# Moving 256 columns at a time in a feed-forward: every wide matmul split in two, and its operands placed anew

## The chip, the cores and the metric

The kernel runs on one core of a Trainium2 chip. The metric is the device time of one execution in microseconds; the median of three runs is shown below. All work is in float32, or in float32 values that are split into an upper part (the value rounded to the matmul type float32r) and a lower part (the rest), so that three float32r matmuls give one product of nearly full precision.

## The reference

Linear attention without a softmax, a root-mean-square norm with a gain, and a feed-forward with SiLU on the 4608 tokens:

```python
kv = np.einsum('bhsd,bhse->bhde', k, v)          # q, k, v: 8 batches, 8 heads, 576 tokens, 64
out = np.einsum('bhsd,bhde->bhse', q, kv)
rms = np.sqrt(np.mean(out * out, axis=-1, keepdims=True) + 1e-06)
x = (out / rms * g_norm).transpose(0, 2, 1, 3).reshape(4608, 512)
h = x @ w_in                                     # 512 x 2048
y = (h / (1 + np.exp(-h))) @ w_out               # 2048 x 512
```

## The kernel before

The tokens are cut into nine blocks of 512 (TN), and the hidden units into 16 groups of 128 (NF), called f. Both weight matrices stay in SBUF as blocks wi0 to wi15 and wo0 to wo15, each with its upper and lower part side by side. Attention for a later batch runs between the feed-forward's steps. The order in which instructions are issued on each engine is that of the program (a manual schedule); jobs of attention are hung on steps by hand.

For each block of tokens and each group f the kernel makes the hidden units (128 units on the partitions, 512 tokens as columns), gates them, and adds their part of the output.

- Blocks 0 and 1: `products` (line 474) makes the hidden units. For each of four quarters c of the 512 inputs, three matmuls: stationary a 128 x 128 piece of wi, moving 512 columns of x. Block 0's x lies in four tiles x0 to x3 (three in "spare" places, x3 in a "late" place), block 1's in x_second.
- Blocks 2 to 8: `pair_step` makes two groups at once with seven Strassen-like products. `product` (line 634) issues six matmuls for each, with 256 moving columns of an operand tile (operands 0 to 3 lie over x_second's place, 4 to 6 in the spare places). A pair step has 42 of these.
- All blocks: `project` (line 505) adds a group's part of the output. Stationary is a 128 x 128 piece of the gated units (gh, the upper part, or gl, the lower), moving are 512 columns of wo. For each of the block's four output tiles of 128 tokens it issues three matmuls: gh by the lower part of wo, gh by its upper part, and gl by the upper part. In the last block the fourth output tile is held in two half banks, so these move 256 columns each. A pair step issues 24 of the wide ones for the two groups of an earlier step (two steps behind).

The gated units are allocated in the pool gp, the weights in the pool weights. Constants and x lie in the pool const, in the order in which they are first asked for. Where a tile starts is therefore set by what stands ahead of it. The kernel before already places one pair of operands on purpose: one tile x_place holds x_second from its start, and the operands of `product` 48 floats (192 bytes) further on.

```python
SHIFT = 48
x_place = const.tile([P, NP * 2 * TN + SHIFT], F32R, name="x_place")
x_second = x_place[:, :NP * 2 * TN].rearrange("p (c a n) -> p c a n", c=NP, a=2)
x_operands = x_place[:, SHIFT:].rearrange("p (c a k n) -> p c a k n", c=NP, a=2, k=2)
```

In this text the distance of a matmul is the start of its moving operand less the start of its stationary operand, modulo 256 bytes.

At the start, `keep_warm` (line 824) issues small matmuls of 128 columns on an identity while the first loads are under way, and GpSimd makes constants: four zeroed tiles, the identity, a permuted identity called both, and the column warm_up that ScalarE reads first.

Of the kernel before, what the change touches and what calls it, by code (L numbers as in the profile page):

```python
# [8 lines left out]
F32 = mybir.dt.float32  # L9
F32R = mybir.dt.float32r  # L10
# [20 lines left out]
def linear_attention_rms_silu_ffn(  # L31
# [22 lines left out]
    nc = tc.nc  # L54
    B, NP, P, S = q.shape
# [3 lines left out]
    TN = 512  # L59
# [5 lines left out]
    const = ctx.enter_context(tc.tile_pool(name="const", bufs=1))  # L65
# [5 lines left out]
    gp = ctx.enter_context(tc.tile_pool(name="gp", bufs=LAG + 1))  # L71
# [2 lines left out]
    ps_at = ctx.enter_context(tc.tile_pool(name="ps_at", bufs=1, space=PSUM))  # L74
    dram = ctx.enter_context(tc.tile_pool(name="dram", bufs=1, space=bass.MemoryType.DRAM))

    kvm = [const.tile([P, P], F32, name=f"kvm{i}") for i in range(NP)]
    for t in kvm:
        nc.gpsimd.memset(t, 0.0)
    ident = const.tile([P, P], F32, name="ident", tag="kh", bufs=2)  # L80
    make_identity(nc, ident)
    warm_up = const.tile([P, 1], F32, name="warm_up")
    nc.gpsimd.memset(warm_up, 1.0)
    gcol = const.tile([P, 1], F32, name="gcol")
    both = const.tile([P, P], F32, name="both", tag="kl", bufs=2)
    nc.gpsimd.tensor_copy(out=both, in_=ident)
    for i in range(4):
        nc.gpsimd.tensor_copy(
            out=both[32 * i:32 * i + 32, 32 * (i ^ 1):32 * (i ^ 1) + 32], in_=ident[32 * i:32 * i + 32, 32 * i:32 * i + 32]
        )  # L90
    d_eps = const.tile([P, 1], F32, name="d_eps")
    nc.gpsimd.memset(d_eps, float(D) * EPS)

    def load_g():
        for h in range(P // D):
            nc.sync.dma_start(out=gcol[h * D:(h + 1) * D, :], in_=g_norm.rearrange("(d o) -> d o", o=1))
# [7 lines left out]

    SHIFT = 48
    x_place = const.tile([P, NP * 2 * TN + SHIFT], F32R, name="x_place")
    x_second = x_place[:, :NP * 2 * TN].rearrange("p (c a n) -> p c a n", c=NP, a=2)
    x_operands = x_place[:, SHIFT:].rearrange("p (c a k n) -> p c a k n", c=NP, a=2, k=2)  # L110
    x_first, lates = {}, {}

    def spare(n, shape, dtype, name):
        return const.tile(shape, dtype, name=name, tag=f"spare{n}")

    def late(n, shape, dtype, name):
        if not lates:
            const.tile([P, 64 - SHIFT], F32, name="gap")
        if name not in lates:
            lates[name] = const.tile(shape, dtype, name=name, tag=f"late{n}")  # L120
        return lates[name]

    def x32(c, w):

        return late(c // 2, [P, 2, TN], F32, f"x32_{c // 2}")[:, c % 2, w]
# [14 lines left out]
    def full_tile(kind, f):  # L140
        if kind == "wo":
            t = late(1, [P, 2, NP * P], F32, "wo_full")[:, f % 2]
        else:
            t = tmp.tile([P, S], F32, name="full", tag="tmp")[:, :NP * P]
        fulls[kind, f] = t
        return t
# [54 lines left out]
    def x_part(t, a, c):  # L201

        if t == 1:
            return x_second[:, c, a]
        if c not in x_first:
            kind = {"shape": [P, 2, TN], "dtype": F32R, "name": f"x{c}"}
            x_first[c] = spare(c, **kind) if c < 3 else late(0, **kind)
        return x_first[c][:, a]
# [248 lines left out]
    def h_bank():  # L457
        return ps_h.tile([P, 512], F32, name="hp", tag="h")
# [6 lines left out]
    def at_bank(tag=None):  # L465

        at_tags.append(at_tags.pop(0))
        return ps_at.tile([P, 512], F32, name="at", tag=tag or at_tags[-1])

    def products(hp, t, f, c):  # L470
        w = parts["wi", f]
        fs = slice(c * P, (c + 1) * P)
        for i, (a, b) in enumerate(((0, 1), (1, 0), (0, 0))):
            nc.tensor.matmul(  # L474
                out=hp[:, :TN], lhsT=w[:, a, fs], rhs=x_part(t, b, c),
                start=(c == 0 and i == 0), stop=(c == NP - 1 and i == 2),
            )

    def gate(t, hp):
# [19 lines left out]
    def project(t, f, gh, gl, bank, n, cs):  # L499
        first, last = order(t)[0], order(t)[-1]  # L500
        w = parts["wo", f]
        ns = slice(n * P, (n + 1) * P)
        bank = bank[:, :cs.stop - cs.start]
        for i, (g, a) in enumerate(((gh, 1), (gh, 0), (gl, 0))):
            nc.tensor.matmul(  # L505
                out=bank, lhsT=g[:, ns], rhs=w[:, a, cs], start=(f == first and i == 0), stop=(f == last and i == 2)
            )
        if f == last:
            ob = tmp.tile([P, S], F32, name="ob", tag="tmp")[:, :cs.stop - cs.start]
            (nc.scalar.copy if n % 2 else nc.vector.tensor_copy)(out=ob, in_=bank)  # L510
            nc.sync.dma_start(out=out[t * TN + n * P:t * TN + (n + 1) * P, cs], in_=ob)
# [9 lines left out]
    def order(t):  # L521

        if t < 2:
            return [(f + t * HF) % NF for f in range(NF)]
        return [f for i in range(HF) for f in (i + HF, i)]
# [69 lines left out]
    def operand(j):  # L595

        if j < 4:
            return x_operands[:, j]
        if j not in operands:
            operands[j] = spare(j - 4, [P, 2, 2, H], F32R, f"operand{j}")  # L600
        return operands[j]
# [20 lines left out]
    def make_operand(m):  # L622
        j, x, _ = seven[m]
        upper, lower = operand(j)[:, 0], operand(j)[:, 1]
        nc.scalar.copy(out=upper, in_=x())
        nc.vector.tensor_tensor(out=lower, in0=x(), in1=upper.bitcast(F32), op=ALU.subtract)

    def product(m, i, out):
        j, _, a_of = seven[m]
        x = operand(j)  # L630
        n = 0
        for c in range(2):
            for a, b in ((0, 1), (1, 0), (0, 0)):
                nc.tensor.matmul(  # L634
                    out=out, lhsT=a_of(i, a, c), rhs=x[:, b, c], start=(n == 0), stop=(n == 5)
                )
                n += 1
# [11 lines left out]
    def pair_step(t, i, groups):  # L649
# [5 lines left out]
        def due(n):  # L655
            while n > 0 and groups:
                n -= (groups[0][-1].stop - groups[0][-1].start) / DM
                project(*groups.pop(0))
# [144 lines left out]
    with tc.manual_schedule():  # L803

        first = [FirstPair(c) for c in range(NP)]
        stats = at_bank().rearrange("p (c i j) -> p c i j", i=2, j=8)
        second = plan(1, 3)
        for item in ORDER.split():
            kind, n = item.rstrip("0123456789"), int(item.lstrip("wiopbg") or 0)
# [30 lines left out]
        def warm_products(c, *fs):  # L840
            if not warm:
                warm.extend([h_bank(), acc_bank()])
            for f in fs:
                products(warm[f], 0, f, c)
# [115 lines left out]
        for t in range(NT):  # L960
# [7 lines left out]
            for step, f in enumerate(order(t)):  # L968
                g = t * NF + step
                for job in first_jobs.pop(g, ()):  # L970
                    job()
                for item in prepped:
                    split_block(*item, nc.scalar.copy)
                prepped = []
                if t == 0:
                    prepped = [("wi", f + 2)] * (3 <= f + 2 < NF) + [("wo", f)] * (f > 0)
                run(sum((bits(*item) for item in prepped), []), *[call() for call in chains.pop(g, ())])
                if t == 0 and 3 < f + 3 < NF:
                    magnitude("wi", f + 3)
                if t == 0 and f < WARM:  # L980
                    hp = warm[f]
                    products(hp, t, f, NP - 1)
                else:
                    hp = h_bank()
                    for c in range(NP):
                        products(hp, t, f, c)
                pend.append(((t, f, *gate(t, hp)), sums))
                if t == 0 and f + 1 < NF:
                    magnitude("wo", f + 1)
                for job in mid_jobs.pop(g, ()):  # L990
                    job()
                if len(pend) > LAG:
                    item, olds = pend.pop(0)
                    for old in olds:
                        project(*item, *old)
                for job in last_jobs.pop(g, ()):
                    job()
# [4 lines left out]
        for old in sums:  # L1002
            for item, _ in pend:
                project(*item, *old)
# [41 lines left out]
```

## Time and profile before

| | before |
|---|---|
| median of 3 runs | 839.12 us (838.94 to 839.2) |
| the profiled execution: its own time | 839.63 us |
| the profiled execution: its span | 837.8 us |
| TensorE matmuls busy | 826.8 us, 5454 instructions |
| TensorE weight loads busy | 734.6 us, 5454 instructions |
| VectorE busy | 528.9 us |
| ScalarE busy | 359.0 us |
| GpSimd busy | 145.9 us |

The span goes from the first to the last instruction; the time of an execution is a little longer. Weight loads overlap the matmuls. Matmuls are pipelined, so the rows of two matmuls that follow each other overlap as well, and the mean length of a row is not what one matmul adds to the time. In the views of the chain of waits a run of matmuls is given from its start to the start of what follows it.

### The profile page before, as it was taken

What the parts mean: (1) busy time and instruction counts of PE and PEld (TensorE: products, weight loads), DVE (VectorE), ACT (ScalarE), POOL (GpSimd) and SP (SyncE); (2) the same over time, 40 slices, a digit from 0 to 9 for tenths busy, and PEclk for the clock granted to TensorE, in tenths of its full rate; (3) what the DMA queues carried; (4) which work ended last, traced back from release to release, by engine and by line L of the source; (5) the groups of instructions that cost most, each with busy time, mean ns of one, the idle gap of its engine ahead of it and who ended that gap; (6) DMA issues with size and microseconds to landing.
All of it is one profiled execution on the core that took longest, in us unless ns stands there. A gap on an engine that the chain in (4) does not pass through costs nothing.

```text
span 837.8 us, 14032 instructions
## 1 busy us (share of the span) xinstructions
PE 826.8 (99%) x5454; PEld 734.6 (88%) x5454; DVE 528.9 (63%) x1027; ACT 359.0 (43%) x744; POOL 145.9 (17%) x142
## 2 busy tenths in 40 slices
PE   8999999999999999999999999999999999999998
PEld 7767888888899999998999998999999999999997
DVE  4886875788476567657766667656865664464332
ACT  3766564534453245325532355225532432243222
POOL 2786983423010002000200011001100000000000
PEclk9999999999999999999999999999999999999999
DMA  8879011337343634364424452444423343334331
GB/s 322 313 257 362 4 57 51 136 145 261 122 161 100 215 115 146 101 214 144 165 91 160 163 173 88 158 158 157 151 84 103 106 155 103 105 102 151 100 102 51
DMA packets 42418, 122.55 MB, mean 146 GB/s; under 512 B 4848, under 2 KB 5104, under 8 KB 42352
## 3 DMA queue, kind: packets, MB, share of 16 engines
q1 hardware_dynamic: 42352, 121.65, 42.4%
q8 instruction: 43, 0.70, 0.4%
q14 instruction: 23, 0.19, 0.1%
HBM read 103.81 MB, written 17.83 MB: 145 GB/s over the span
## 4 chain that ended last, share of the span: by engine, by line
PE 94%; DMA 4%; POOL 1%; ACT 0%; issue 0%; SPq 0%
PE acc L505 46%; PE hp L634 33%; PE hp L474 9%; PE at L253 2%; DMA k<-in_k 1%; DMA wo<-in_moe_w_out 1%; DMA early_wi<-in_v 1%; DMA v<-in_v 1%; PE at L289 1%; PE at L288 1%; PE at L290 1%; PE at L505 1%; DMA wi<-in_moe_w_in 1%; PE at L286 1%; POOL wo L191 0%
## 5 line engine op out<-in xcount | busy, mean ns | idle before, releaser
L505 PE MATMUL acc<-wo,gh 128*128 128x512 f32 (+1 forms) x1152 | 354.1, 389 | 0.1
L505 PEld LDWEIGHTS acc<-wo,gh 128*128 128x128 f32 x1152 | 210.3, 188 | 39.7 <-POOL wo L191 0.3
L505 PE MATMUL acc<-wo,gl 128*128 128x512 f32 x576 | 223.0, 387 | 0.5 <-POOL gl L485 0.5
L634 PE MATMUL hp<-x_place,wi 128*128 128x256 f32 x1344 | 167.8, 280 | 0.0
L634 PEld LDWEIGHTS hp<-x_place,wi 128*128 128x128 f32 x1344 | 162.0, 189 | 0.0
L634 PEld LDWEIGHTS hp<-operand,wi 128*128 128x128 f32 x1008 | 126.0, 189 | 3.9
L505 PEld LDWEIGHTS acc<-wo,gl 128*128 128x128 f32 x576 | 108.1, 188 | 23.5 <-POOL gl L485 0.9
L634 PE MATMUL hp<-operand,wi 128*128 128x256 f32 x1008 | 127.5, 281 | 0.0
L275 POOL TENSOR_TENSOR ql<-q,qh 128x576 fp32r<-128x576 f32 x24 | 35.6, 1483 | 376.0 <-ACT qh L274 341.9
L685 ACT COPY wi<-hp 128x256 f32<-128x256 f32 x56 | 20.9, 373 | 140.9 <-PE hp L634 140.9
L643 ACT ACTIVATE gh<-gf 128x512 fp32r<-128x512 f32 x56 | 35.4, 633 | 94.4 <-DVE gf L698 81.6
L643 ACT ACTIVATE gh<-wi 128x512 fp32r<-128x512 f32 x56 | 35.5, 634 | 79.8 <-DVE wi L698 68.0
L686 DVE TENSOR_TENSOR gf<-hp,wi 128x256 f32<-128x256 f32 x28 | 11.9, 425 | 84.8 <-ACT wi L685 84.8
L686 DVE TENSOR_TENSOR wi<-hp,wi 128x256 f32<-128x256 f32 x28 | 11.9, 424 | 84.3 <-ACT wi L685 84.3
L474 PE MATMUL hp<-x,wi 128*128 128x512 f32 x180 | 46.4, 402 | 1.4 <-POOL wi L191 1.4
L474 PE MATMUL hp<-x_place,wi 128*128 128x512 f32 x192 | 46.4, 390 | 0.0
L647 DVE TENSOR_TENSOR gl<-wi,gh 128x512 fp32r<-128x512 f32 x56 | 38.4, 685 | 11.4 <-ACT wi L644 11.4
L687 DVE TENSOR_TENSOR wi<-hp,wi 128x256 f32<-128x256 f32 x56 | 23.8, 425 | 32.3 <-PE hp L634 32.3
L647 DVE TENSOR_TENSOR gl<-gf,gh 128x512 fp32r<-128x512 f32 x56 | 39.0, 696 | 7.3 <-ACT gf L644 7.3
L294 ACT ACTIVATE sq<-at 128x288 f32<-128x288 f32 x56 | 22.9, 410 | 45.6 <-PE at L290 38.9
L474 PEld LDWEIGHTS hp<-x_place,wi 128*128 128x128 f32 x192 | 35.7, 188 | 7.3
L316 DVE SCALAR_TENSOR_TENSOR x<-o,gcol,yT 128x128 f32<-128x128 f32 (+7 forms) x52 | 40.7, 784 | 1.9
(142 smaller groups left out, 1006.8 us busy)
## 6 DMA issues: line engine op xcount, KB each, us to landing
wi<-sums_in_dram SPq DMA_DIRECT2D x112, 512.0 KB, 3.3
out<-ob SPq DMA_DIRECT2D x35, 256.0 KB, 2.4
wi<-in_moe_w_in SPq DMA_DIRECT2D x16, 512.0 KB, 7.8
wo<-in_moe_w_out SPq DMA_DIRECT2D x16, 512.0 KB, 8.9
sums_in_dram<-sum_parts SPq DMA_DIRECT2D x16, 512.0 KB, 2.6
k<-in_k SPq DMA_DIRECT2D x28, 288.0 KB, 5.2
v<-in_v SPq DMA_DIRECT2D x28, 288.0 KB, 5.4
q<-in_q SPq DMA_DIRECT2D x28, 288.0 KB, 4.0
```

What stands on the lines that cost most here:

```text
L253: nc.tensor.matmul(out=self.kv[h], lhsT=self.k[rows, c, :], rhs=self.v[rows, c, :], start=(start and r == 0), stop=(stop and r == 4),)
L275: nc.gpsimd.tensor_tensor(out=self.ql, in0=self.q, in1=self.qh.bitcast(F32), op=ALU.subtract)
L294: nc.scalar.activation(out=self.sq[:, self.w], in_=self.ps, func=AF.Square)
L316: nc.vector.scalar_tensor_tensor(out=to, in0=self.o[:, a:e], scalar=gcol, in1=self.yT, op0=ALU.mult, op1=ALU.mult)
L474: nc.tensor.matmul(out=hp[:, :TN], lhsT=w[:, a, fs], rhs=x_part(t, b, c), start=(c == 0 and i == 0), stop=(c == NP - 1 and i == 2),)
L505: nc.tensor.matmul(out=bank, lhsT=g[:, ns], rhs=w[:, a, cs], start=(f == first and i == 0), stop=(f == last and i == 2))
L634: nc.tensor.matmul(out=out, lhsT=a_of(i, a, c), rhs=x[:, b, c], start=(n == 0), stop=(n == 5))
L643: nc.scalar.activation(out=gh, in_=x, func=AF.Silu)
L647: nc.vector.tensor_tensor(out=gl, in0=x, in1=gh.bitcast(F32), op=ALU.subtract)
L685: nc.scalar.copy(out=p1, in_=u)
L686: nc.vector.tensor_tensor(out=c1[:, low], in0=v, in1=p1, op=ALU.add)
L687: nc.vector.tensor_tensor(out=u2, in0=y, in1=p1, op=ALU.add)
```

## The change

Every feed-forward matmul that moved 512 columns becomes two of 256 columns, with the same stationary operand, into the two halves of the same bank. A new function `halves` issues them; the first half of the first matmul of a sum carries the start flag, and the second half of the last one the stop flag. `products` and `project` call it. Half-bank sums of 256 columns stay single matmuls. `product` is not touched.

Tiles move: a gap of 64 bytes is put ahead of the gated units; x_second becomes a tile of its own behind a gap of 192 bytes, and the operands 0 to 3 lie in it without a shift; a gap of 64 bytes stands ahead of the late tiles, as before. The two one-column constants warm_up and gcol are allocated behind both, and a gap of 32 bytes is added, so that what follows starts on a multiple of 256 bytes. The memset of warm_up is issued behind the copies that make both.

```diff
+    gp.tile([P, 16], F32, name="gap_before_gated", bufs=1)
     kvm = [const.tile([P, P], F32, name=f"kvm{i}") for i in range(NP)]
...
-    warm_up = const.tile([P, 1], F32, name="warm_up")
-    nc.gpsimd.memset(warm_up, 1.0)
-    gcol = const.tile([P, 1], F32, name="gcol")
     both = const.tile([P, P], F32, name="both", tag="kl", bufs=2)
...
+    warm_up = const.tile([P, 1], F32, name="warm_up")
+    nc.gpsimd.memset(warm_up, 1.0)
+    gcol = const.tile([P, 1], F32, name="gcol")
     d_eps = const.tile([P, 1], F32, name="d_eps")
     nc.gpsimd.memset(d_eps, float(D) * EPS)
+    const.tile([P, 8], F32, name="gap")
...
     SHIFT = 48
-    x_place = const.tile([P, NP * 2 * TN + SHIFT], F32R, name="x_place")
-    x_second = x_place[:, :NP * 2 * TN].rearrange("p (c a n) -> p c a n", c=NP, a=2)
-    x_operands = x_place[:, SHIFT:].rearrange("p (c a k n) -> p c a k n", c=NP, a=2, k=2)
+    const.tile([P, SHIFT], F32, name="gap_before")
+    x_second = const.tile([P, NP, 2, TN], F32R, name="x_second")
...
-            const.tile([P, 64 - SHIFT], F32, name="gap")
+            const.tile([P, 64 - SHIFT], F32, name="gap_behind")
...
+    def halves(to, stationary, moving, start, stop):
+        n = to.shape[-1]
+        for at in range(0, n, 256):
+            nc.tensor.matmul(
+                out=to[:, at:at + 256], lhsT=stationary, rhs=moving[:, at:at + 256],
+                start=start and at == 0, stop=stop and at == n - 256,
+            )
+
     def products(hp, t, f, c):
...
-            nc.tensor.matmul(
-                out=hp[:, :TN], lhsT=w[:, a, fs], rhs=x_part(t, b, c),
-                start=(c == 0 and i == 0), stop=(c == NP - 1 and i == 2),
+            halves(
+                hp[:, :TN], w[:, a, fs], x_part(t, b, c), c == 0 and i == 0, c == NP - 1 and i == 2
             )
...
-            nc.tensor.matmul(
-                out=bank, lhsT=g[:, ns], rhs=w[:, a, cs], start=(f == first and i == 0), stop=(f == last and i == 2)
-            )
+            halves(bank, g[:, ns], w[:, a, cs], f == first and i == 0, f == last and i == 2)
...
-            return x_operands[:, j]
+            return x_second[:, j].rearrange("p a (k n) -> p a k n", k=2)
```

## Rows read from the trace of the kernel before

**Rows 1.** The page: TensorE's busy time, and its granted clock in 40 slices.
```profile
PE 826.8 (99%) x5454; PEld 734.6 (88%) x5454; DVE 528.9 (63%) x1027; ACT 359.0 (43%) x744; POOL 145.9 (17%) x142
...
PEclk9999999999999999999999999999999999999999
```

**Rows 2.** Windows: stretch, length, busy time (instructions) of each engine, clock, DMA.
```profile
45.00:222.00 177.00, 174.18 (x952) 142.16 (x951) 129.66 (x216) 91.25 (x198) 94.33 (x85) 1.00 0.43 158
222.00:685.00 463.00, 463.00 (x3213) 421.65 (x3212) 302.29 (x623) 194.32 (x409) 29.33 (x20) 1.00 0.43 141
```

**Rows 3.** Groups by line and form: busy us, mean ns of one, idle before.
```profile
L505 PE MATMUL acc<-wo,gh 128*128 128x512 f32 x1120 | 347.8, 392 | 0.1
L505 PE MATMUL acc<-wo,gl 128*128 128x512 f32 x560 | 218.5, 390 | 0.5 <-POOL gl L485 0.5
L634 PE MATMUL hp<-x_place,wi 128*128 128x256 f32 x1344 | 167.8, 280 | 0.0
```

**Rows 4.** Chain of waits, 720 to 742 us: start, us, what.
```profile
720.04 5.44 PE acc L505 x24
725.49 4.95 PE hp L634 x42
```

**Rows 5.** Chain of waits, 331 to 350 us, around attention matmuls.
```profile
331.31 2.83 PE hp L634 x24
334.14 0.13 PE at L288
334.27 0.14 PE at L289
...
334.54 2.06 PE hp L634 x18
...
337.00 2.09 PE acc L505 x9
```

**Rows 6.** Chain of waits, 765 to 790 us, in the last block.
```profile
766.76 0.36 PE at L505 x3
767.12 4.78 PE hp L634 x42
```

**Rows 7.** Timeline of TensorE, 767 to 780 us: start, us, group.
```profile
769.02 2.88 PE L634 MATMUL hp<-x_place,wi 128*128 128x256 f32 x24
771.74 0.63 PE L505 MATMUL acc<-wo,gh 128*128 128x512 f32 x2
```

**Rows 8.** Groups of the page: loads of the stationary operand for gh.
```profile
L505 PEld LDWEIGHTS acc<-wo,gh 128*128 128x128 f32 x1152 | 210.3, 188 | 39.7 <-POOL wo L191 0.3
```

**Rows 9.** Chain shares by line: 222 to 685, 685 to 767, 767 to 838 us.
```profile
by line: PE acc L505 49.3%; PE hp L634 45.0%; PE at L253 2.3%; PE at L289 1.2%; PE at L288 1.2%; PE at L290 1.1%
...
by line: PE acc L505 52.3%; PE hp L634 47.0%; PE at L505 0.7%
...
by line: PE acc L505 47.6%; PE hp L634 40.4%; PE at L505 7.5%; ACT ob L510 0.5%; issue 0.0%
```

**Rows 10.** Chain of waits, 95 to 136 us: blocks 0 and 1.
```profile
106.81 2.79 PE hp L474 x12
109.59 2.73 PE acc L505 x12
...
126.21 2.72 PE hp L474 x12
128.93 2.72 PE acc L505 x12
```

**Rows 11.** Timeline of all engines, 0 to 14 us.
```profile
2.03 0.20 ACT L828 ACTIVATE warm_up<-warm_up 128x1 f32<-128x1 f32 x1
...
2.31 0.94 POOL L88 COPY both<-ident 32x32 f32<-32x32 f32 x4
...
7.63 0.43 ACT L261 COPY kvm<-hp 64x64 f32<-64x64 f32 x2 [5.40 <-PE hp L253]
...
9.10 1.95 PE L824 MATMUL hp<-ident 128*128 128x128 f32 x16
```

## The prediction

> **What bounds the kernel now.** I read the page first: TensorE is busy for 826.8 of 837.8 us with a granted clock of 9 tenths or more in every slice (the 2.4 GHz level); VectorE, the next engine, for 63% [rows 1]. The windows by stage say where the rest lies: from 45 to 222 us TensorE stands idle for 2.8 us, and from 222 us, where the Strassen blocks begin, not at all [rows 2]. So the time is the distance from one matmul's start to the next, summed. A busy time can't show that distance, since one matmul's row lasts 280 or 390 ns [rows 3] while the next has long begun. The chain of waits can: on it a run of matmuls lasts from one start to the next, and a run divided by its count is the price of one move. On that view everything below rests.
>
> In an undisturbed step the 24 output matmuls of 512 columns (L505) take 5.44 us, 226.7 ns each, and the 42 products of 256 columns (L634) take 4.95 us, 117.9 ns each [rows 4]. Two narrow moves thus cost 235.7 ns where one wide one costs 226.7. But the narrow ones have a second rhythm. Around the attention matmuls, 24 products before them take 2.83 us (117.9 each) and the 18 behind them 2.06 us (114.4, with the transition) [rows 5]. In the last token block all 42 take 4.78 us [rows 6], and once the rhythm stands, the 24 that begin at 769.02 are over at 771.74, where the next group begins: 113.3 ns each [rows 7]. Twice 113.3 is 226.7, the price of the wide move. The change lives on which of the two rhythms holds.
>
> The operands are the same in both. By the tile sizes, x_place holds 16384 bytes and 192 more, the gap behind it 64, and the tiles from there to the weights are multiples of 256; so weights begin at x_place's remainder modulo 256, and the operands of L634 stand 192 behind them in either rhythm. What differs is what ran before. Behind a run of wide moves at distance 0 the products take 4.95 us [rows 4]. Behind attention matmuls of 288 columns [rows 5], or behind half-bank matmuls of 256 columns at distance 0 (0.36 us for three, 120 ns each) [rows 6], they fall into 113.3 and stay there until the next wide run. I see no entry into the slow rhythm but from wide moves.
>
> **The change part by part.** *The split.* The wide moves are 1120 and 560 of L505 [rows 3] and, by the loops, 2 blocks of 16 units of 12, 384, of L474; each becomes two, 2064 more matmuls. Each brings its own load of the stationary operand: a group's two gh matmuls follow each other on the same 128 columns, and there are 1152 loads for 1152 matmuls [rows 8], so the second half will load again. Issue should keep up, as L634 already runs at this pace.
>
> *The distance.* Gated tiles begin 64 bytes on, so wo stands 64 before them, which is 192 modulo 256; x_second begins 192 on. Only the fourth quarter of the first block's x (x3, a late tile) stays at distance 0. Then nearly every feed-forward matmul is a 256-column move at distance 192, the form with the two rhythms, and the wide runs, the only thing seen to lead into the slow one, are gone. I take 113.3, because what is left ahead of it (288 columns, or 256 at distance 0) led there each time.
>
> The sum, term by term:
> - L634: 40 of its 56 steps are slow (4.95), 10 mixed (2.83 + 2.06), 6 fast (4.78): 275.6 us. 2352 at 113.3 are 266.6: **-9.0**.
> - L505 from 222 us on: 49.3% of 463, 52.3% of 82 and 47.6% of 71 us of the chain [rows 9], 304.9 in all; without its 48 half-bank matmuls at 0.12, 299.1 for 1310 wide moves. What lies above 226.7 are runs around attention (2.09 us for 9) [rows 5]. At 226.7 they are 297.0: **-2.1**.
> - The 96 half-bank matmuls, 120 to 113.3: **-0.6**.
> - L505 before 222 us: 12 take 2.73 us in the first block, 2.72 in the second [rows 10]; with the waits near the start about **-0.4** for some 15 runs.
> - L474: in the first block 9 of 12 stand at distance 192 and 3 at 0, 2.79 us [rows 10]. Split, 18 at 113.3 and 6 at 120 are 2.76: -0.03 in 16 steps, **-0.5**. In the second block 12 take 2.72 already: 0.
>
> Together -12.6 us, and all of it on the path, since TensorE is never idle from 222 us on [rows 2] and the other engines' work, 63% at most, fits a step that is 2% shorter.
>
> *Moved tiles.* The memset of warm_up goes behind the copies of both, which end at 3.25 us; ACT's first use of it slips from 2.03 to about 3.3, and its next work starts at 7.63 [rows 11]: nothing, and 1.2 us if that cover were gone. The attention operands' distances change too; 144 matmuls of 0.13 to 0.14 us [rows 5] bound it at 0.7 us either way, and between these I take 0.
>
> *Bounds of one narrow move.* Above: 120 ns, the half-bank matmuls [rows 6]. Below: 110 ns, the 16 warming matmuls of 128 columns, each with its own load (1.95 us less 0.3 for the last one's row, over 15) [rows 11]; such a move hides nothing but its load. The operands now begin 32 bytes off a multiple of 64 and then on one, so a price between 110 and 113.3 isn't excluded. I take 113.3, which the same form shows.
>
> The wide move at 226.7 and twice the fast narrow one at 226.7 show no charge per matmul that a split would pay again. The Trainium skill's page "TensorE: Matmul & The Clock Gate" (section "Back-to-back issue gap") puts a matmul at its columns over 2.4 GHz and some 2.5 ns more, which speaks against a split: by it 2064 more matmuls would cost an estimated 5.2 us. The trace differs from that rule, as neither 226.7 nor 117.9 comes out of it.
>
> The profiled execution took 839.63 us, 1.8 more than its span; the median of the runs is 839.12. From the one -12.6 gives 827.0, from the other 826.5; I say 826.5.
>
> **Rivals.**
> - *The slow rhythm holds (slower).* Narrow moves at distance 192 keep 117.9, say because the two halves share a stationary operand, or because attention at its new distances leads into it. For: 40 of 56 steps run so now [rows 4], and none lets go by itself within 42 matmuls. Against: each entry seen is a wide run. Price: L634 +1.7; L505 from 222 us 308.8 against 299.1, +9.7, and before, 354 at 235.7 against some 227.5, +2.9; L474 +0.8 and +1.7; half-banks -0.2: +16.6, **855.7 us**. It decides from 43% of the moves on, where -12.6 + 29.2 s crosses zero.
> - *A price per move.* 512 columns at 226.7 and 256 at 120, both at distance 0, differ by 106.7 for 256 columns; that leaves 13.3 ns per move, and if the new distance doesn't remove it for wo and the gated tiles, each split pays it twice. All at 120: L634 +6.6, L505 +15.3 and +4.4, L474 +1.4 and +2.6: +30.3, **869.4 us**. Against: 113.3 at distance 192 [rows 7]. The page's charge named above has this sign.
> - *Both rhythms alternate:* 37% to 49% of the moves slow end within 0.2% of **839 us**.
> - *The load is the limit, 110 ns.* L634 -16.9, L505 -10.9 and -2.7, L474 and half-banks -4.7: -35.2, **804 us**; halfway there, 815.
>
> **How the numbers follow.** The fast rhythm, with at most a third of the moves slow, 0.55, its own range 821 to 836. Near the load's limit 0.06. Alternating about zero 0.07. Slow rhythm 0.25. A price per move 0.07. Faster by over 0.2% (about what a measurement of this kernel can tell from no change) is then 0.61, the same 0.07, slower 0.32. The range goes from halfway to the load's limit, 815, to just past the slow rhythm, 856.5; some 0.05 stay below it and 0.08 above.
>
> **What would show it.** On the chain 42 products take 4.76 us in every step, and the 48 output matmuls that replace 24 take 5.44. PE and PEld counts rise by 2064 each. If L634 stays at 4.95 and a run of 48 takes 5.66, the step on the rhythm is wrong; if 42 take 4.62, the load's limit is met; if L634 is fast and the 48 take 5.76, the price per move was real for wo. A new wait of PE for a gated tile, or attention matmuls off 0.13 to 0.14 us, would be a step I missed.

## The result, and the profile after

The changed kernel takes 841.63 us against 839.16 before: 1.003 times as long, 95% interval 1.002 to 1.004. It is slower by 0.3%, where 826.5 us was forecast. One of its eight executions took 2119.7 us and is left out of the ratio.

The page has the 2064 additional matmuls, each with its load, and the loads now fill the span:

```profile
span 840.0 us, 18181 instructions
...
PE 830.0 (99%) x7518; PEld 823.1 (98%) x7518; DVE 529.3 (63%) x1027; ACT 358.5 (43%) x744; POOL 146.0 (17%) x142
```

As before, TensorE never stands idle in the Strassen blocks; this is the window from 222 to 685 us, whose columns are those of [rows 2]:

```profile
222.00:685.00 463.00, 463.00 (x4212) 461.95 (x4211) 302.98 (x624) 193.85 (x409) 29.38 (x20) 1.00 0.42 141
```

So the chain of waits has the answer again: start, length, what, and how many. First an undisturbed step (the products are now line 645, the output matmuls line 479), against [rows 4]; then the end of block 2 and the first step of block 3; then a stretch around attention, against [rows 5]; then the second block of tokens, against [rows 10].

```profile
690.00 5.65 PE acc L479 x48
695.65 4.78 PE hp L645 x42
...
301.79 2.63 PE at L257 x80
304.41 5.66 PE acc L479 x48
310.07 4.95 PE hp L645 x42
...
331.18 1.41 PE acc L479 x12
332.59 2.74 PE hp L645 x24
335.33 0.13 PE at L292
...
338.18 2.06 PE acc L479 x18
...
187.44 2.83 PE acc L479 x24
190.27 2.74 PE hp L479 x24
```

The reader is to see two rhythms in one step, and that they have changed places. The products, 4.95 us in 40 of 56 steps before, take 4.78: that part of the forecast came. The output matmuls take 5.65 us for 48, 117.7 ns each, where 24 wide ones took 5.44. A quiet step, one without attention, is 10.43 us, and was 10.39. Around attention most of the output matmuls run fast, 18 in 2.06 us; the 12 behind the last group take 1.41, 117.5 ns each. In the first step of block 3, behind 80 small matmuls of attention's first stage, it is the other way about: the products take 4.95, and the output matmuls ahead of them are fast from the seventh on. The timeline shows that; of its rows here are the one that begins with the seventh matmul and the one that follows the run:

```profile
305.15 0.62 PE L479 MATMUL acc<-wo,gh 128*128 128x256 f32 x4
...
309.91 1.34 PE L645 MATMUL hp<-operand,wi 128*128 128x256 f32 x10
```

These are 42 matmuls from 305.15 to 309.91 us, 4.76 us, 113.3 ns each.

The chain's shares from the first product of block 2 to the end, before and after:

```profile
by line: PE acc L505 49.5%; PE hp L634 44.7%; PE at L253 1.7%; PE at L505 0.9%; PE at L289 0.9%; PE at L288 0.9%; PE at L290 0.9%; ACT ob L510 0.1%; issue 0.0%
```

```profile
by line: PE acc L479 50.8%; PE hp L645 43.6%; PE at L257 1.7%; PE at L479 0.9%; PE at L293 0.9%; PE at L294 0.9%; PE at L292 0.9%; ACT ob L521 0.1%; issue 0.0%
```

Of 615.5 us before and 616.2 after these are 304.7 and 313.0 us of output matmuls, 275.1 and 268.6 of products: some +8 against some -6.5. Before that point lie 222.3 and 223.8 us, +1.5: in the second block 24 output matmuls take 2.83 us and 24 of x 2.74, where 12 wide ones took 2.72 each.

### The profile page after: what moved, and what is told of

It reads as the page before. It is cut to its first block, busy times and chain, and to the rows that moved or that the text cites. A ratio compares the mean times of both kernels' runs of the same rounds, so it can differ in the third digit from the quotient of the medians.

```text
span 840.0 us, 18181 instructions
## 1 busy us (share of the span) xinstructions
PE 830.0 (99%) x7518; PEld 823.1 (98%) x7518; DVE 529.3 (63%) x1027; ACT 358.5 (43%) x744; POOL 146.0 (17%) x142
## 4 chain that ended last, share of the span: by engine, by line
PE 94%; DMA 4%; POOL 1%; issue 0%; ACT 0%; SPq 0%
PE acc L479 47%; PE hp L645 32%; PE hp L479 9%; PE at L257 2%; DMA wo<-in_moe_w_out 1%; DMA k<-in_k 1%; DMA v<-in_v 1%; PE at L293 1%; PE at L294 1%; PE at L292 1%; DMA early_wi<-in_v 1%; PE at L479 1%; DMA wi<-in_moe_w_in 1%; PE at L290 1%; POOL wo L195 0%
## 5 line engine op out<-in xcount | busy, mean ns | idle before, releaser
L479 PE MATMUL acc<-wo,gh 128*128 128x256 f32 x2272 | 360.8, 281 | 0.0
L479 PEld LDWEIGHTS acc<-wo,gh 128*128 128x128 f32 x2272 | 307.3, 189 | 1.0 <-POOL wo L195 0.3
L479 PE MATMUL acc<-wo,gl 128*128 128x256 f32 x1136 | 226.8, 280 | 0.5 <-POOL gl L498 0.5
L479 PEld LDWEIGHTS acc<-wo,gl 128*128 128x128 f32 x1136 | 174.1, 189 | 0.7 <-POOL gl L498 0.7
L645 PE MATMUL hp<-x_second,wi 128*128 128x256 f32 x1344 | 163.7, 277 | 0.0
L645 PEld LDWEIGHTS hp<-x_second,wi 128*128 128x128 f32 x1344 | 158.0, 188 | 0.0
L645 PE MATMUL hp<-operand,wi 128*128 128x256 f32 x1008 | 124.7, 277 | 0.0
L645 PEld LDWEIGHTS hp<-operand,wi 128*128 128x128 f32 x1008 | 119.9, 188 | 0.0
L479 PE MATMUL hp<-x,wi 128*128 128x256 f32 x360 | 46.4, 283 | 1.5 <-POOL wi L195 1.5
L479 PE MATMUL hp<-x_second,wi 128*128 128x256 f32 x384 | 46.7, 278 | 0.0
L479 PEld LDWEIGHTS hp<-x,wi 128*128 128x128 f32 x360 | 43.3, 188 | 2.4 <-POOL wi L195 1.7
L479 PEld LDWEIGHTS hp<-x_second,wi 128*128 128x128 f32 x384 | 45.3, 188 | 0.1
```

Of the source, the lines that this page charges most:

```text
L479: nc.tensor.matmul(out=to[:, at:at + 256], lhsT=stationary, rhs=moving[:, at:at + 256], start=start and at == 0, stop=stop and at == n - 256,)
L645: nc.tensor.matmul(out=out, lhsT=a_of(i, a, c), rhs=x[:, b, c], start=(n == 0), stop=(n == 5))
```

## The experiments

Two theories, formed on the profile after. The **carried rhythm**: a narrow move at distance 192 has both rhythms, it goes on in the one it is in, and the rhythm is set at a passage, where one family of matmuls (output matmuls or products) follows the other, by how the last moving operand stands to the next stationary one. In the changed kernel that distance is 128 from products to output matmuls (x at 192, gated units at 64) and 0 on the way back (wo at 0, wi at 0). The rival is the **own form**: the output matmuls are slow by themselves, because two or four in a row use one stationary operand, or because of their places.

**One distance everywhere.** wo gets a pool of its own, 192 bytes on, and the gated units go to 0, so stationary operands all stand at 0 and moving ones at 192 (but for x3 of the first block, at 0). Against the changed kernel:

```diff
+    weights_o = ctx.enter_context(tc.tile_pool(name="weights_o", bufs=1))
...
-    gp.tile([P, 16], F32, name="gap_before_gated", bufs=1)
+    weights_o.tile([P, 48], F32, name="gap_before_wo", bufs=1)
+    kvq.tile([P, 16], F32, name="gap_before_kvq", bufs=1)
...
-        return weights.tile([P, 2, NP * P], dtype, name=f"{kind}{f}", tag=f"{kind}{f}")
+        pool = weights_o if kind == "wo" else weights
+        return pool.tile([P, 2, NP * P], dtype, name=f"{kind}{f}", tag=f"{kind}{f}")
...
-        return weights.tile([P, S], F32, name=f"early_{name}", tag=name)
+        pool = weights_o if name[:2] == "wo" else weights
+        return pool.tile([P, S], F32, name=f"early_{name}", tag=name)
```

> The output weights wo move to 192 modulo 256 and the gated units to 0, so that every stationary operand of the feed-forward stands at 0 and every moving one at 192: the distance inside the output runs stays 192 as in the changed kernel, and it is now 192 as well where output matmuls and products follow each other (there it was 128 going in and 0 coming out). Entry theory (the rhythm is carried over and only a change of distance between the two families, or attention, alters it): 48 output matmuls take 5.44 to 5.48 us instead of 5.65, 42 products 4.76 to 4.78, median 826 to 829 us. Own-form theory (output matmuls are slow because two halves in a row use the same stationary operand): 48 stay at 5.65, products stay fast, 840 to 842 us.

Measured: 827.48 us, 0.986 (0.9845 to 0.9875). The chain of this run, in a quiet step, behind the 80 small matmuls, and around attention:

```profile
699.58 5.44 PE acc L483 x48
705.02 4.76 PE hp L649 x42
...
300.40 5.66 PE acc L483 x48
...
316.26 2.72 PE hp L649 x24
318.98 0.13 PE at L295
...
319.38 2.06 PE hp L649 x18
...
321.83 2.04 PE acc L483 x18
```

The narrow moves are fast, 113.3 ns, but for the first few of some runs behind attention (5.66 for 48, 2.06 for 18). The halves still share a stationary operand, so that part of the own form is out.

**Only the products moved.** The output matmuls keep the changed kernel's places (gated at 64, wo at 0); wi goes to 64 and x to 0, which makes the distance 192 everywhere too. Against the changed kernel, again with a pool for wo:

```diff
+    weights_o.tile([P, 48], F32, name="gap_before_wo", bufs=1)
...
-    const.tile([P, SHIFT], F32, name="gap_before")
...
+        pool = weights_o if kind == "wo" else weights
...
```

> The output matmuls keep exactly the places of the changed kernel (gated units at 64, wo at 0); instead the products' stationary wi moves to 64 and x to 0, so their own distance stays 192 and the distance at both changes of family becomes 192. Entry theory: the same as with all operands at 0 and 192, 48 output matmuls in 5.44 to 5.48 us, median 826 to 829 us. A theory by which the places 64 and 0 of the output matmuls themselves are bad, or the shared stationary operand: 48 stay at 5.65, 840 to 842 us.

Measured: 848.84 us, 1.0114 (1.0099 to 1.0129). Both theories missed the time, the own form by less. The chain says why; from the first output run of the Strassen blocks on:

```profile
218.31 5.44 PE acc L482 x48
223.75 4.76 PE hp L648 x42
228.51 2.72 PE acc L482 x24
231.23 2.72 PE hp L648 x24
233.95 0.13 PE at L294
...
236.81 2.12 PE acc L482 x18
...
255.42 4.95 PE hp L648 x42
260.37 5.65 PE acc L482 x48
...
302.77 2.63 PE at L259 x80
305.39 5.66 PE acc L482 x48
311.05 4.76 PE hp L648 x42
315.81 5.44 PE acc L482 x48
...
596.89 2.12 PE acc L482 x18
...
838.10 4.95 PE acc L482 x42
```

The places are not slow: up to 233 us both families run at 113.3 ns. Then attention puts them into 117.7, and, with one distance at every passage, nothing takes them out again: the whole block stays slow until the 80 small matmuls for the next one. Behind the last of these, attention leads into the slow rhythm at 596.89 us, and it holds to the last run, 42 in 4.95 us, at the end of the kernel. The rhythm is carried, the slow one as well as the fast. What I had left out is that attention sets it too.

**The fast version, 64 bytes further on.** This puts the feed-forward where the last run had it, modulo 256 bytes, and lets attention's operands move along. Against the version with one distance:

```diff
+    const.tile([P, 16], F32, name="gap_at_head", bufs=1)
     kvm = [const.tile([P, P], F32, name=f"kvm{i}") for i in range(NP)]
```

> The version with one distance, everything 64 bytes further on: the feed-forward's operands then stand exactly where they stood in the run that moved the products only (stationary at 64, moving at 0, 192 apart everywhere), but attention's operands move along, so that the last attention matmul stands to the next stationary operand as in the version with one distance. If the rhythm is carried over as it comes, and attention is what put that run into the slow one: 48 output matmuls in 5.44, 42 products in 4.76, 827 to 829 us. If the places 64 and 0 themselves are slow: 5.65 and 4.95, 846 to 850 us.

Measured: 827.63 us, 0.9861 (0.9846 to 0.9876); 48 output matmuls in 5.44, 42 products in 4.76. With the same operands in the same places modulo 256 bytes, 21 us lie between the two runs. Between their programs stand attention's places against the feed-forward's and what else moved along; the chain above puts the change of rhythm at attention.

**The passages exchanged.** wo at 128 and the gated units at 192: inside the runs still 192, from products to output 0, and back 128. Against the changed kernel, with a pool for wo as above:

```diff
-    gp.tile([P, 16], F32, name="gap_before_gated", bufs=1)
+    gp.tile([P, 48], F32, name="gap_before_gated", bufs=1)
+    weights_o.tile([P, 32], F32, name="gap_before_wo", bufs=1)
+    kvq.tile([P, 32], F32, name="gap_before_kvq", bufs=1)
...
```

> wo at 128 and the gated units at 192: inside the runs all distances stay 192, but going from products to output matmuls the distance is now 0 (it was 128) and coming back 128 (it was 0). Entry theory, from the changed kernel's own boundaries (128 ends in the slow rhythm, 0 turns the rhythm over): the two families change places, 48 output matmuls in 5.44 to 5.50 us and 42 products in 4.95; against the changed kernel about -14 us for the output matmuls and +9 for the products, median 835 to 838 us. Own-form theory: nothing changes, 48 at 5.65 and 42 at 4.78, 841 us.

```profile
708.20 4.95 PE hp L650 x42
713.14 5.46 PE acc L484 x48
```

Measured: 843.46 us, 1.0052 (1.0037 to 1.0067). The families did change rhythms, as the carried rhythm says and the own form doesn't. My sum was off: it counted a gain for every output matmul, though those around attention were fast already in the changed kernel. A quiet step is 10.41 us here against 10.43, and around attention 18 output matmuls take 2.12 us, where they took 2.06.

**The split alone,** with the places of the kernel before.

> The kernel before with its places, and only the split: output matmuls of 256 columns at distance 0, products at 192 as before. By the half-bank matmuls of the kernel before, distance 0 costs 120 ns a move: 48 output matmuls 5.76 us, and behind them the products fall into the fast rhythm, 42 in 4.78. Sum against before: +15 and +4 for the output matmuls, about +4 for the first two blocks, -8 for the products: 852 to 856 us. If the distance doesn't matter to the output matmuls: 841 us as the changed kernel.

Measured: 852.37 us, 1.0157 (1.014 to 1.0174). A quiet step, in the chain:

```profile
699.14 5.74 PE acc L475 x48
704.88 4.78 PE hp L641 x42
```

The output matmuls cost 119.6 ns at distance 0, and behind them the products are fast.

**The places alone,** with the moves of 512 columns left whole.

```diff
     def halves(to, stationary, moving, start, stop):
-        n = to.shape[-1]
...
+        nc.tensor.matmul(out=to, lhsT=stationary, rhs=moving, start=start, stop=stop)
```

> The changed kernel's places without the split: output matmuls of 512 columns at distance 192. From the first block of the kernel before (12 matmuls, nine of them at 192, in 2.79 us) one wide move at 192 costs about 234 ns against 226.7 at 0: 24 output matmuls 5.60 to 5.65 us, L505 +11 us, second block's x +1.3. Products behind them: fast (4.78) gives 842 to 845 us, slow (4.95) 850 to 853 us; no row tells which.

Measured: 846.58 us, 1.0087 (1.0072 to 1.0102), between the two sums, since the products of quiet steps are slow and fast in turn:

```profile
699.57 4.95 PE hp L638 x42
704.52 5.60 PE acc L475 x24
710.12 4.78 PE hp L638 x42
```

A wide move at 192 costs 233 ns, against 226.7 at 0; a narrow one costs 119.6 at 0, and 113.3 or 117.7 at 192. So either half of the change alone costs more than both.

**The kernel before, with three of 24 wide moves split.** Only the last output tile of each pair step goes in halves, at distance 0; `project` takes the width as step.

```diff
-                project(*groups.pop(0))
+                project(*groups.pop(0), step=256 if len(groups) == 0 else TN)
...
```

> The kernel before, places unchanged; only the last output tile of each pair step (three of 24 wide matmuls) is split into 256 columns at distance 0. Entry theory: as in the last block of the kernel before, half-width matmuls at distance 0 lead the products into the fast rhythm, 42 in 4.78 us in every step, while each step pays 3 x 13.3 ns for the split: -7 us and +2, median 833 to 835 us. If the fast rhythm of the last block had another cause (less traffic, no attention): 840 to 842 us.

```profile
216.38 5.44 PE acc L508 x24
221.82 4.95 PE hp L638 x42
...
704.37 5.49 PE acc L508 x27
709.86 4.78 PE hp L638 x42
```

Measured: 833.97 us, 0.9937 (0.9922 to 0.9952). The products of every quiet step but the first are fast, at the price of 0.05 us; the first, at 221.82 us, follows a run of 24 that ends unsplit, and takes 4.95. What runs last before them sets the rhythm, with nothing moved.

**Other distances.** The version with one distance, at 128, 64, 224 and 160 in place of 192; shown is the edit for 128, the others have 16, 56 and 40 floats, and the gap in kvq fills up to 256 bytes.

```diff
-    weights_o.tile([P, 48], F32, name="gap_before_wo", bufs=1)
-    kvq.tile([P, 16], F32, name="gap_before_kvq", bufs=1)
+    weights_o.tile([P, 32], F32, name="gap_before_wo", bufs=1)
+    kvq.tile([P, 32], F32, name="gap_before_kvq", bufs=1)
...
-    SHIFT = 48
+    SHIFT = 32
```

> As the version with one distance, but the one distance is 128 instead of 192 (all stationary at 0, all moving at 128). If it is enough that the distance is the same everywhere: 826 to 829 us. If 192 itself is needed, each narrow move costs more than 113.3 ns, up to the 120 of distance 0: up to 868 us; the 288-column attention matmuls at 128 (0.13 us each) don't tell.

> The version with one distance, at 64 instead of 192 (all stationary at 0, all moving at 64). The narrow move cost 113.3 ns at 192, about 118.7 at 128 and 120 at 0; if the price depends on the distance alone and 192 is the only good one, 118 to 120 again and 858 to 868 us; if 64 were as good as 192, 827 us.

> The same at 224. If 192 lies inside a good stretch that goes on to 224: 113.3 ns or less, down to the 110 of the warming matmuls, 805 to 828 us; if 192 is the edge of it: 116 to 120 ns, 845 to 868 us.

> The same at 160, on the other side of 192. Good stretch: 805 to 828 us; edge: 845 to 868 us.

Measured: 860.69 us at 128 (1.0256, 1.0239 to 1.0273), 854.09 at 64 (1.0178, 1.0149 to 1.0208), 858.34 at 224 (1.0229, 1.0199 to 1.0259), 857.8 at 160 (1.0223, 1.0193 to 1.0252). A quiet step's runs in the chain, one fence for each, in this order:

```profile
705.63 5.70 PE acc L483 x48
711.33 4.98 PE hp L649 x42
```

```profile
700.18 5.65 PE acc L483 x48
705.84 4.95 PE hp L649 x42
```

```profile
703.82 5.68 PE acc L483 x48
709.50 4.96 PE hp L649 x42
```

```profile
702.83 5.70 PE acc L483 x48
708.52 4.98 PE hp L649 x42
```

All lie between 117.7 and 118.8 ns a move in a quiet step. Of the distances tried, 0, 64, 128, 160, 192 and 224, only 192 showed 113.3 in a whole quiet step. But 64 has the fast price as well: in that version the output matmuls behind one group of attention matmuls in each of four blocks take 2.04 us for 18, 113.3 each, and those behind the next 2.12, 117.8 each.

```profile
330.24 2.04 PE acc L483 x18
...
332.69 2.12 PE acc L483 x18
```

Each of these fast runs ends at attention matmuls, and the next is slow. So 854.09 us is the time of 64 with the slow rhythm nearly throughout; whether the fast one would hold there in a quiet step, no run shows.

## Why the prediction was wrong

*What held.* The bound (TensorE's starts), the two rhythms, the counts, the bounds of one move, the moved memset that costs nothing (though not as told: GpSimd still runs it at 1.44 us, ahead of the copies, and ScalarE reads warm_up at 2.02) and the products: their -9.0 came as some -6.5, 4.78 us a step instead of 4.76, since the first few moves of a run are still slower, and in four blocks the first step stayed at 4.95. The price of distance 0, taken as 120, came out at 119.6. The split shows no charge for each additional matmul: the run with one distance has the same 2064 more and is faster than the kernel before by some 11.8 us. That TensorE is never idle from 222 us on was read from rows that end at 685; the trace bears it out up to the last matmul, which ends at 834.6.

*The step that failed* is the one on the distance: "I take 113.3, because what is left ahead of it (288 columns, or 256 at distance 0) led there each time." The list of what is left ahead was incomplete. The most frequent predecessor of an output run is a run of products, and that passage, from x at 192 to gated units at 64, has a distance of its own, 128, that no row of before shows: there both families had their stationary operands at one remainder. I priced the distance within each run and not between runs. The term for L505 from 222 us on, forecast at -2.1, came as some +8, and the second block's 0 and the first block's small gains as +1.5 together. The run with one distance takes away just this and lands at 827.48, a microsecond above the forecast. Most of that microsecond is four runs of 48 behind the 80 small matmuls, 5.66 us each where 5.44 was forecast; in the kernel before they took 5.71, and what they had above 5.44 was about half of the 2.1 us that the prediction put down to the runs around attention.

*The sentence under it* was wrong as well: that there is no entry into the slow rhythm but from wide moves. Output runs enter it from fast products at 128, and attention led into it in the run that moved the products only.

*Of the rivals,* none had the mechanism. The time lies near the one that I gave to alternating rhythms, just outside its 0.2%: by the prediction's own -12.6 + 29.2 s the measured +2.5 us are 52% of the moves slow. But these do not alternate by chance: 41 of the 45 runs of 48 output matmuls are slow, and 42 of the 46 runs of 42 products fast. Nor did any sign name the pair of 4.78 for the products and 5.65 for the 48. The shared stationary operand of the first rival is ruled out by the run with one distance. That rival also named attention's distances as a possible cause, which the pair of runs at the same operands, 848.84 and 827.63, bears out as a danger, though in the changed kernel attention led mostly into the fast rhythm.

*Left open:* why a distance of 128 leads into the slow rhythm while 0 turns it over, which of attention's places lead where, and what happens inside TensorE in either. The runs show at which passages the rhythm changes, not what changes it. In the versions with narrow moves at 192 the distance at a passage and the shift of the operands from one family to the other are also one number, so the runs do not tell which of the two counts.

## What to carry to other kernels

Where matmuls follow each other without a gap, price them from start to start, by runs on the chain of waits, and look for more than one price of the same form. Give all stationary operands one remainder modulo 256 bytes and all moving ones another, so that the passages between families have the same distance as the runs. Try several distances, since with the same care 128 took 860.69 us and 192 827.48. Then look at what else runs between the families (here attention), since a rhythm once lost stayed lost for a whole block. A change of width and a change of place belong together: of 0 and 192, 512 columns ran faster at 0 and 256 at 192, and each change alone cost more than both.

## What was unexpected of the hardware

The same 256-column matmul on the same operands costs 113.3 or 117.7 ns by what ran before it, and kept the price over hundreds of moves: in the run that moved the products only the slow one held from the attention at 236.81 us to the small matmuls at 302.77, and in the last blocks from 596.89 us to the end, some 245 us. A split of three matmuls in each step, with everything else in its place, made the kernel 0.6% faster.
